# Sink-and-window attention with two mixture-of-experts layers on one core: keys and queries of a pair of heads are turned and split behind the scores of the preceding pair

## Chip, core and metric

The kernel runs on one core of a Trainium2 chip. The metric is the device time of one execution in microseconds (us). It is measured as the median of several runs; the profile is one further execution, with its own time.

The engines of a core work from their own in-order instruction streams: TensorE (PE, matmuls and transposes into PSUM; its weight loads are listed as PEld), VectorE (DVE), ScalarE (ACT), GpSimd (POOL) and SyncE (SP), whose queue issues most DMAs here. Semaphores hold an instruction until what it reads is there.

## What is computed

```python
def _attn_ref(q, k, v, n_sink, window):            # q, k, v: [4, 8, 768, 64]
    scores = scale * np.matmul(q, k.transpose(0, 1, 3, 2))
    is_sink = pos[None, :] < int(n_sink)           # 4 sinks
    rel = pos[:, None] - pos[None, :]
    in_window = (rel >= 0) & (rel < int(window))   # window 128
    scores = np.where(is_sink | in_window, scores, -1000000000.0)
    scores = scores - np.max(scores, axis=-1, keepdims=True)
    a = np.exp(scores)
    a = a / (np.sum(a, axis=-1, keepdims=True) + 1e-09)
    return np.matmul(a, v)
...
def _moe_ref(x, w_in, w_out):                      # 3072 tokens, 512 -> 2048 -> 512
    h = x @ w_in
    g = np.where(h >= 1, h, np.where(h <= -1, 0.0, (h + 1) ** 2 / 4))
    return g @ w_out
...
def reference(**kwargs):
    x = attention, heads side by side: [3072, 512]
    x = _moe_ref(x)
    return _moe2_ref(x)    # 8 experts, each takes its 384 best tokens: relu(x @ w1) @ w2
```

The code is shortened, and the last function is told in words.

## The kernel before

**Tiling.** The 3072 tokens are 12 blocks of 256 (two tiles of 128), three blocks per batch; blocks 0, 3, 6 and 9 begin a batch (`first`, t0 = 0) and have the sinks' loads besides. In a block attention goes over four pairs of heads. Precision comes from splitting a float32 operand into a high and a low part and adding two or three matmuls. Blocks 0 and 1 take `attn_steps_f32`, which turns keys and queries by TensorE transposes (L482, L498); blocks 2 to 11 take `attn_steps`, which turns them by VectorE. Each block's output x is the input of the first dense MoE (`moe1_steps`: `hid` L632, activation L640 to L644, `proj` L657), which runs in between the attention of later blocks; the second MoE follows from about 775 us on.

**The steps of a pair in `attn_steps`.** `load_kq` issues four DMAs for k and eight for q on SP (L427, in `load_blocks`), `load_v` two for v (L276) and, in a first block, four for the sinks' rows (L284). `trans_k` turns k by a VectorE stream transpose (L431), copies its high part on ScalarE (L303), makes the low one on VectorE (L304) and adds the sinks (L308, L309). `trans_q` does the same: transpose (qr, L431), high part sq on ScalarE (L317), low part ql on VectorE (L318). `s00` to `s11` are the scores: two matmuls each (sc, L335 with ql, L336 with sq), the maximum on VectorE (L338), the exponential on ScalarE (L340). `norm` takes the reciprocal on VectorE (L345, L346) and multiplies the probabilities on GpSimd (pr; L354, and L349 and L351 in first blocks). `ptrans` turns them on TensorE (tp, L373) with their high and low part on ScalarE (pt, L375) and VectorE (pt, L376); `strans` does so for the sinks' part. `pv` multiplies with the values (xp, L392), `split` makes x (xa: L398 on ScalarE, L399 on VectorE; then L408 or L411, L412, L413), `split_v` splits the values (L289, L290), `sinks` the sinks' rows (svt L591, L592; sv L596).

**What sets the order.** `pipeline` (L599 to L614) writes the steps of one stage after the other: a stage belongs to a pair, "+" names steps of the next pair and "*" of the one after it. A plan spreads the stages over time among the MoE steps by weights (the steps named in `idle` weigh nothing, except `trans_k` and `trans_q` of blocks 0 and 1, which are on TensorE), and that gives the program's order. The framework's scheduler then orders the instructions of each engine by what is ready and by that program order, so it can already hoist a step past its neighbours. The raw tiles of k, q and v, and ks, sq and ql, have one buffer each; pr, pt and the split values two.

Of the kernel before, what the change touches and what calls it, by code (L numbers as in the profile page):

```python
# [74 lines left out]
class Kernel:  # L75
# [524 lines left out]
    def pipeline(self, pairs):  # L600

        idle = {"load_kq", "load_v", "trans_k", "trans_q", "norm0", "norm1", "split_v", "sinks", "split"}

        def steps(order, now, nxt, far):
            of = {"": now, "+": nxt, "*": far}
            found = [(of[s.rstrip("abcdefghijklmnopqrstuvwxyz_0123456789")], s.lstrip("+*")) for s in order.split()]
            return [(0.0 if s in idle and s not in d.get("on_pe", ()) else 1.0, d[s]) for d, s in found if d and d[s]]

        out = [steps("load_kq load_v trans_k trans_q +load_kq split_v sinks +load_v s00 s01 norm0 s10 s11 norm1",
                     pairs[0], pairs[1], None)]  # L610
        for now, nxt, far in zip(pairs, pairs[1:] + [None], pairs[2:] + [None, None]):
            out.append(steps("+trans_k +trans_q *load_kq ptrans0 ptrans1 strans +s00 +s01 +norm0 pv0 +s10 +s11 +norm1 "
                             "pv1 +split_v +sinks *load_v split", now, nxt, far))
        return out  # L614


# [763 lines left out]
def tile_sink_window_attention__moe__expert_choice(ctx, tc, q, k, v, n_sink, window, w_in, w_out, wg, w1, w2, out):  # L1380
# [10 lines left out]
    def pipeline(general):  # L1391
        with ExitStack() as c0:
# [72 lines left out]
            plan.run()  # L1465

    pipeline(False)
    flag = nc.values_load(K.flag[0:1, 0:1], min_val=0, max_val=1)
    with tc.If(flag):
        with ExitStack() as c0:  # L1470
            K.attn_general(c0.enter_context, xg)
        pipeline(True)
# [32 lines left out]
```

## Time and profile before

| what | before |
|---|---|
| median of 3 runs | 1196.77 us (1194.34 to 1202.54) |
| the profiled execution: time | 1197.53 us |
| the profiled execution: span from first to last instruction | 1195.6 us |
| mean granted TensorE clock, of full speed | 0.976 |
| TensorE busy | 1112.3 us, 93% of the span |
| VectorE busy | 858.5 us, 72% |
| ScalarE busy | 704.2 us, 59% |
| GpSimd busy | 485.5 us, 41% |

The busy times are sums over the whole span, and 2 us lie outside of it. Where TensorE is nearly always busy, a wait of its own counts in full, and one of another engine only if it reaches TensorE. The rows behind the change show waits in the form "engine line waited for: us in total, times, longest us", and a timeline's row has its idle time and what released it in brackets.

### The profile page before, as it was taken

To read this page: it belongs to the slowest core of one execution; us is meant where nothing else is said; L and a number is where in the kernel's file an instruction comes from. 1 tells how busy PE (TensorE), PEld (TensorE's weight loads), DVE (VectorE), ACT (ScalarE), POOL (GpSimd) and SP (SyncE) were. 2 spreads that over 40 slices of the span, in tenths; PEclk is the share of its full clock that TensorE was granted. 3 is DMA by queue.
4 is the path that set the end of the run, shared out by engine and by line. 5 is a ranking of instruction groups with operands and counts; after the bars stand their busy time and mean duration, and the time that the engine had idled before them with its cause. 6 is when DMAs were issued, how large, how long until landed. Compare 5 with 4: busy or idle time off the path is not lost.

```text
span 1195.6 us, 24202 instructions
## 1 busy us (share of the span) xinstructions
PE 1112.3 (93%) x8256; PEld 1027.9 (86%) x8256; DVE 858.5 (72%) x2578; ACT 704.2 (59%) x1602; POOL 485.5 (41%) x588
## 2 busy tenths in 40 slices
PE   5898989999999999999999999999699999999995
PEld 3677878999999999999998999999578788878994
DVE  6778878777777876776777787755788787878330
ACT  5787767666667666775666676642345434444551
POOL 1335645454555444455544455541222222322321
PEclk9899989999999999999999999999799999999998
DMA  4555522323222122222122322000667767677861
GB/s 113 132 154 166 159 50 55 65 48 75 47 55 40 34 55 49 56 50 58 33 52 49 69 42 57 11 19 1 185 173 200 204 168 208 189 192 194 227 176 41
DMA packets 241926, 118.11 MB, mean 99 GB/s; under 512 B 196096, under 2 KB 220672, under 8 KB 241792
## 3 DMA queue, kind: packets, MB, share of 16 engines
q1 hardware_dynamic: 233200, 86.58, 28.5%
q0 software_dynamic: 8592, 29.89, 10.7%
q8 instruction: 67, 1.10, 0.4%
q14 instruction: 67, 0.55, 0.2%
HBM read 86.00 MB, written 13.11 MB: 83 GB/s over the span
## 4 chain that ended last, share of the span: by engine, by line
PE 54%; DVE 10%; issue 8%; ACT 5%; POOL 4%; DMA 3%; SPq 1%; DVEq 0%; POOLq 0%; ACTq 0%
PE up L657 14%; PE hp L632 14%; PE hp L1054 8%; PE us L1081 7%; PE xp L392 2%; PE tp L373 2%; PE sc L335 2%; PE sc L336 1%; DVE ks L304 1%; POOL pr L354 1%; PE pk L955 1%; DVE ind L804 1%; SPq L427 1%; POOL gl L644 1%; PE pg L819 1%
## 5 line engine op out<-in xcount | busy, mean ns | idle before, releaser
L644 POOL TENSOR_TENSOR gl<-u,gh 128x256 fp32r<-128x256 f32 x192 | 148.9, 776 | 210.1 <-ACT gh L643 159.3
L657 PE MATMUL up<-woh,gl 128*128 128x256 f32 (+1 forms) x576 | 167.1, 290 | 2.0 <-POOL gl L644 1.7
L657 PE MATMUL up<-wol,gh 128*128 128x256 f32 (+1 forms) x576 | 164.6, 286 | 0.6 <-DVE wol L231 0.6
L657 PE MATMUL up<-woh,gh 128*128 128x256 f32 x576 | 164.3, 286 | 0.0
L641 ACT ACTIVATE u<-u,half 128x256 f32<-128x256 f32 x192 | 98.0, 510 | 89.6 <-DVE u L640 82.3
L632 PE MATMUL hp<-xh,wil 128*128 128x256 f32 x768 | 132.3, 291 | 3.8 <-ACT xh L412 1.9
L632 PE MATMUL hp<-xl,wih 128*128 128x256 f32 x768 | 125.9, 284 | 0.7 <-POOL xl L413 0.5
L632 PE MATMUL hp<-xh,wih 128*128 128x256 f32 x768 | 126.0, 285 | 0.0
L657 PEld LDWEIGHTS up<-woh,gl 128*128 128x128 f32 x576 | 109.8, 191 | 3.8 <-POOL gl L644 2.3
L632 PEld LDWEIGHTS hp<-xh,wil 128*128 128x128 f32 x768 | 107.4, 191 | 6.2 <-ACT xh L412 2.9
L657 PEld LDWEIGHTS up<-wol,gh 128*128 128x128 f32 x576 | 109.4, 190 | 1.2 <-DVE wol L231 0.8
L657 PEld LDWEIGHTS up<-woh,gh 128*128 128x128 f32 x576 | 109.4, 190 | 0.7 <-issue 0.7
L632 PEld LDWEIGHTS hp<-xl,wih 128*128 128x128 f32 x768 | 106.7, 191 | 1.9 <-POOL xl L413 1.5
L632 PEld LDWEIGHTS hp<-xh,wih 128*128 128x128 f32 x768 | 107.2, 193 | 0.0
L642 DVE TENSOR_TENSOR u<-hp,u 128x256 f32<-128x256 f32 x192 | 80.8, 421 | 33.6 <-ACT u L641 31.9
L640 DVE TENSOR_SCALAR u<-hp 128x256 f32<-128x256 f32 x192 | 80.2, 418 | 34.4 <-PE hp L632 29.3
L354 POOL TENSOR_TENSOR pr<-pr,sm 128x576 f32<-128x576 f32 x56 | 69.3, 1238 | 68.9 <-DVE sm L346 34.6
L340 ACT ACTIVATE pr<-pr,sm 128x288 f32<-128x288 f32 (+1 forms) x160 | 85.5, 535 | 18.3 <-DVE sm L338 17.4
L643 ACT CAST gh<-u 128x256 fp32r<-128x256 f32 x192 | 77.7, 405 | 27.0 <-DVE u L642 24.0
L1062 ACT ACTIVATE hh<-hp 128x384 fp32r<-128x384 f32 x64 | 31.5, 492 | 102.9 <-PE hp L1054 88.3
L376 DVE TENSOR_TENSOR pt<-tp,pt 128x512 fp32r<-128x512 f32 (+1 forms) x80 | 51.5, 647 | 41.8 <-ACT pt L375 41.1
L1081 PE MATMUL us<-w2h,hl 128*128 128x512 f32 x192 | 80.8, 421 | 0.0
(270 smaller groups left out, 3047.8 us busy)
## 6 DMA issues: line engine op xcount, KB each, us to landing
w1r<-in_moe_w_dram SPq DMA_DIRECT2D x32, 512.0 KB, 4.4
w2r<-in_moe_w_dram SPq DMA_DIRECT2D x32, 512.0 KB, 4.6
w2l<-w2r POOLq DMA_DIRECT2D x32, 512.0 KB
qr<-in_q_dram SPq DMA_DIRECT2D x320, 32.0 KB, 2.0
dr<-in_moe_w_in_dram SPq DMA_DIRECT2D x16, 512.0 KB, 4.1
dr<-in_moe_w_out_dram SPq DMA_DIRECT2D x16, 512.0 KB, 4.4
x2d<-ev SPq DMA_DIRECT2D x26, 256.0 KB, 2.2
kr<-in_k_dram SPq DMA_DIRECT2D x112, 48.0 KB, 2.2
```

The lines of the kernel that those rows point to most:

```text
L340: nc.scalar.activation(pr, pr, AF.Exp, bias=sm[:, 0, u:u + 1], scale=-1.0, accum_out=sm[:, 1, u:u + 1])
L354: nc.gpsimd.tensor_tensor(out=pr, in0=pr, in1=r.unsqueeze(2).to_broadcast([P, 2, 2 * P + NS]), op=OP.mult)
L376: nc.vector.tensor_tensor(out=pt[:, 1, :n], in0=ps, in1=pt[:, 0, :n].bitcast(F32), op=OP.subtract)
L632: nc.tensor.matmul(ps, w_[:, k, fs], x_[:, k, :], start=(i == 0 and k == 0), stop=(i == 2 and k == 3))
L640: nc.vector.tensor_scalar(u, ps, -1.0, 1.0, op0=OP.max, op1=OP.min)
L641: nc.scalar.activation(u, u, AF.Square, bias=self.half, scale=0.5)
L642: nc.vector.tensor_tensor(out=u, in0=ps, in1=u, op=OP.max)
L643: nc.scalar.copy(gh, u)
L644: nc.gpsimd.tensor_tensor(out=gl, in0=u, in1=gh.bitcast(F32), op=OP.subtract)
L657: nc.tensor.matmul(o, g_[:, ts], self.w_out_part(w_, f)[:, cs], start=(f == fa and i == 0 and (cs.start > 0 or t == 0)), stop=(f == fz - 1 ...
L1054: nc.tensor.matmul(ps, w_[:, k, fs], x_[:, k, :], start=(i == 0 and k == 0), stop=(i == 2 and k == 3))
L1081: nc.tensor.matmul(us[j], h_[:, o], w_[:, f % 2, :], start=(f == 0 and i == 0), stop=(f == nf - 1 and i == 2))
```

## The change

`trans_k` and `trans_q` of a pair, which stood at the head of the preceding pair's stage beside that pair's transposes, now stand one stage earlier, right behind the last scores and the norm of the pair before (ahead of `pv1`, `split_v` and `load_v`). `load_kq`, which refills their tiles, moves along with them and is now of the third pair ahead ("^"). The first group of steps gets the three for its pairs as well. Nothing within a step changes. In the changed kernel lines after 613 have numbers that are 2 higher (L640 is L642 there).

```diff
-        def steps(order, now, nxt, far):
-            of = {"": now, "+": nxt, "*": far}
-            found = [(of[s.rstrip("abcdefghijklmnopqrstuvwxyz_0123456789")], s.lstrip("+*")) for s in order.split()]
+        def steps(order, now, nxt, far, last):
+            of = {"": now, "+": nxt, "*": far, "^": last}
+            found = [(of[s.rstrip("abcdefghijklmnopqrstuvwxyz_0123456789")], s.lstrip("+*^")) for s in order.split()]
             return [(0.0 if s in idle and s not in d.get("on_pe", ()) else 1.0, d[s]) for d, s in found if d and d[s]]
 
-        out = [steps("load_kq load_v trans_k trans_q +load_kq split_v sinks +load_v s00 s01 norm0 s10 s11 norm1",
-                     pairs[0], pairs[1], None)]
-        for now, nxt, far in zip(pairs, pairs[1:] + [None], pairs[2:] + [None, None]):
-            out.append(steps("+trans_k +trans_q *load_kq ptrans0 ptrans1 strans +s00 +s01 +norm0 pv0 +s10 +s11 +norm1 "
-                             "pv1 +split_v +sinks *load_v split", now, nxt, far))
+        out = [steps("load_kq load_v trans_k trans_q +load_kq split_v sinks +load_v s00 s01 norm0 s10 s11 norm1 "
+                     "+trans_k +trans_q *load_kq",
+                     pairs[0], pairs[1], pairs[2], None)]
+        for now, nxt, far, last in zip(pairs, *(pairs[i:] + [None] * i for i in (1, 2, 3))):
+            out.append(steps("ptrans0 ptrans1 strans +s00 +s01 +norm0 pv0 +s10 +s11 +norm1 "
+                             "*trans_k *trans_q ^load_kq "
+                             "pv1 +split_v +sinks *load_v split", now, nxt, far, last))
```

What stands in the engines' streams is the scheduler's doing, so three places follow as they stand there.

VectorE at the end of block 6, behind the second half's scores of its third pair and ahead of the first scores of its fourth (qr and ql are that pair's queries, ks and sk its keys; pt and xa belong to the pair before). Before:

```order
L345 TENSOR_SCALAR sm<-sm 128x2
L346 RECIPROCAL sm<-sm 128x2
L304 TENSOR_TENSOR ks<-kr,ks 64x2x128
L431 STREAM_TRANSPOSE qr<-qr 128x512
L399 TENSOR_TENSOR xa<-xp,xa 64x384
L592 TENSOR_TENSOR svt<-vr,svt 128x64
L308 CAST sk<-ks 128x64
L376 TENSOR_TENSOR pt<-tp,pt 128x384
L596 TENSOR_SCALAR sv<-svt,par 128x128 x2
L309 CAST ks<-sk 128x2x32
L318 SCALAR_TENSOR_TENSOR ql<-qr,sq 128x512
```

In the changed kernel:

```order
L431 STREAM_TRANSPOSE qr<-qr 128x512
L642 TENSOR_SCALAR u<-hp 128x256
L338 ISA pr,sm<-sc,m_129 128x288
L338 ISA sm 128x1
L304 TENSOR_TENSOR ks<-kr,ks 64x2x128
L644 TENSOR_TENSOR u<-hp,u 128x256
L345 TENSOR_SCALAR sm<-sm 128x2
L346 RECIPROCAL sm<-sm 128x2
L304 TENSOR_TENSOR ks<-kr,ks 64x2x128
L308 CAST sk<-ks 128x64
L309 CAST ks<-sk 128x2x32
L318 SCALAR_TENSOR_TENSOR ql<-qr,sq 128x512
```

The transpose of the queries moved from behind the reciprocal to ahead of the last maximum, and ql now stands ahead of xa, svt, pt and sv, which follow these rows.

VectorE in block 3, behind the keys of its third pair. Before:

```order
L304 TENSOR_TENSOR ks<-kr,ks 64x2x128
L308 CAST sk<-ks 128x64
L309 CAST ks<-sk 128x2x32
L399 TENSOR_TENSOR xa<-xp,xa 64x384
L431 STREAM_TRANSPOSE qr<-qr 128x512
L640 TENSOR_SCALAR u<-hp 128x256
L318 SCALAR_TENSOR_TENSOR ql<-qr,sq 128x512
L642 TENSOR_TENSOR u<-hp,u 128x256
```

In the changed kernel:

```order
L304 TENSOR_TENSOR ks<-kr,ks 64x2x128
L308 CAST sk<-ks 128x64
L309 CAST ks<-sk 128x2x32
L399 TENSOR_TENSOR xa<-xp,xa 64x384
L642 TENSOR_SCALAR u<-hp 128x256
L376 TENSOR_TENSOR pt<-tp,pt 128x384
L644 TENSOR_TENSOR u<-hp,u 128x256
L431 STREAM_TRANSPOSE qr<-qr 128x512
L376 TENSOR_TENSOR pt<-tp,pt 128x384
L592 TENSOR_TENSOR svt<-vr,svt 128x64
L318 SCALAR_TENSOR_TENSOR ql<-qr,sq 128x512
```

Here qr has moved behind a pt and ql behind two of them and svt; on TensorE the scores that read ql stand six up matmuls (L657) further back.

SyncE's queue in block 9 (kr, qr: keys and queries; vr: values and sinks). Before:

```order
L427 DMA kr<-in_k_dram 32x8x32 x4
L427 DMA qr<-in_q_dram 32x8x32 x2
L276 DMA vr<-in_v_dram 128x2x64 x2
L284 DMA vr<-in_v_dram 32x64 x4
L427 DMA qr<-in_q_dram 32x8x32 x6
```

In the changed kernel:

```order
L427 DMA kr<-in_k_dram 32x8x32 x4
L427 DMA qr<-in_q_dram 32x8x32 x8
L276 DMA vr<-in_v_dram 128x2x64 x2
L284 DMA vr<-in_v_dram 32x64 x4
L427 DMA kr<-in_k_dram 32x12x32 x4
```

All eight transfers of the queries now stand ahead of the values' six.

## Rows read from the trace of the kernel before

**Rows 1.** Windows: stretch, length, busy PE PEld DVE ACT POOL, clock, DMA share, GB/s.

```profile
0.00:200.00 200.00, 169.87 (x1086) 146.06 (x1087) 154.87 (x443) 143.41 (x352) 86.16 (x97) 0.93 0.46 121
200.00:775.00 575.00, 550.10 (x4494) 542.81 (x4494) 434.85 (x1220) 385.60 (x979) 290.38 (x362) 1.00 0.26 50
```

**Rows 2.** TensorE's waits from 200 to 775 us: total us, times, longest.

```profile
PE tp L373 <- POOL pr L354: 13.4, 11, 1.9
PE sc L335 <- DVE ql L318: 7.7, 6, 2.1
PE hp L632 <- ACT xh L412: 1.9, 3, 1.1
```

**Rows 3.** Timeline, TensorE: start us, us, instruction, idle before and its releaser.

```profile
277.68 0.40 PE L335 MATMUL sc<-ks,ql 128*128 128x288 f32 x1 [1.48 <-DVE ql L318]
...
446.88 0.33 PE L335 MATMUL sc<-ks,ql 128*128 128x128 f32 x1 [2.07 <-DVE ql L318]
...
464.59 0.40 PE L335 MATMUL sc<-ks,ql 128*128 128x288 f32 x1 [1.17 <-DVE ql L318]
...
634.40 0.33 PE L335 MATMUL sc<-ks,ql 128*128 128x128 f32 x1 [0.99 <-DVE ql L318]
...
650.38 0.40 PE L335 MATMUL sc<-ks,ql 128*128 128x288 f32 x1 [1.13 <-DVE ql L318]
```

**Rows 4.** Timeline, VectorE, ahead of the scores at 446.88.

```profile
442.88 0.71 DVE L431 STREAM_TRANSPOSE qr<-qr 128x512 f32<-128x512 f32 x1 [1.18 <-DMA qr<-in_q_dram]
443.62 0.55 DVE L399 TENSOR_TENSOR xa<-xp,xa 64x384 f32<-64x384 f32 x1
444.20 0.23 DVE L592 TENSOR_TENSOR svt<-vr,svt 128x64 fp32r<-128x64 f32 x1
...
444.72 0.55 DVE L376 TENSOR_TENSOR pt<-tp,pt 128x384 fp32r<-128x384 f32 x1
445.19 0.94 DVE L596 TENSOR_SCALAR sv<-svt,par 128x128 fp32r<-128x128 f32 x2
...
446.15 0.68 DVE L318 SCALAR_TENSOR_TENSOR ql<-qr,sq 128x512 fp32r<-128x512 f32 x1
```

**Rows 5.** Timeline, SyncE's DMA issues, the loads ahead of those scores.

```profile
433.10 0.91 SPq L276 DMA_DIRECT2D vr<-in_v_dram  x2
434.05 2.39 SPq L284 DMA_DIRECT2D vr<-in_v_dram  x4
436.49 3.05 SPq L427 DMA_DIRECT2D qr<-in_q_dram  x6
```

**Rows 6.** Timeline, block 3: VectorE and TensorE at two pairs' first scores.

```profile
233.37 0.69 DVE L318 SCALAR_TENSOR_TENSOR ql<-qr,sq 128x512 fp32r<-128x512 f32 x1 [0.70 <-ACT sq L317]
...
234.82 0.22 PE L335 MATMUL sc<-ks,ql 128*128 128x128 f32 x1
...
246.88 0.52 PE L373 MATMUL tp<-ident,pr 128*128 128x128 f32 x3
...
248.68 0.22 PE L335 MATMUL sc<-ks,ql 128*128 128x128 f32 x1
```

**Rows 7.** Timeline, GpSimd: one pr by itself, one beside a ql.

```profile
312.82 1.16 POOL L354 TENSOR_TENSOR pr<-pr,sm 128x576 f32<-128x576 f32 x1 [0.81 <-DVE sm L346]
...
319.10 1.59 POOL L354 TENSOR_TENSOR pr<-pr,sm 128x576 f32<-128x576 f32 x1 [3.79 <-DVE ks L309]
```

**Rows 8.** The first 200 us: TensorE's waits, and a window (columns of rows 1).

```profile
PE gp L219 <- DVE df L247: 4.1, 6, 1.6
PE gg L227 <- ACT gw L221: 3.1, 2, 2.9
PE up L657 <- POOL wql L249: 2.2, 2, 1.4
...
30.00:40.00 10.00, 9.35 (x38) 6.39 (x38) 9.16 (x38) 8.37 (x25) 4.34 (x8) 0.66 0.42 84
```

**Rows 9.** ScalarE's waits from 200 to 775 us: the cast of the values.

```profile
ACT v L289 <- DMA vr<-in_v_dram: 5.4, 6, 1.6
```

## The prediction

> **What bounds the kernel now.** I read three views, in this order. The table of windows says where TensorE has something to lose or to win [rows 1]. Between 200 and 775 us, where nearly all of attention runs in between the first MoE, TensorE is busy 550.10 of 575 us at a granted clock of 1.00: it bounds this part, it has 24.9 us of idle time, and nothing is to be won from the clock. VectorE, ScalarE and GpSimd are busy 435, 386 and 290 us of it and have slack on average. In the first 200 us TensorE idles 30.1 us at a clock of 0.93. After 775 us no step of attention is left.
>
> TensorE's waits in 200 to 775 us [rows 2] name two steps of attention as nearly the whole: transposes of the probabilities (tp) that wait for GpSimd's normalisation (pr), 13.4 us in 11 waits, and scores (sc) that wait for VectorE's low half of the queries (ql), 7.7 us in 6. The change moves what makes ql; it doesn't move what makes pr. So 7.7 us is about all that it can take out of the steady part directly.
>
> The timeline gives five of the six waits by place [rows 3]: 1.48, 2.07, 1.17, 0.99 and 1.13, together 6.84 us. They stand where a block with t0 = 0 ends and the next begins: for block 6 the last pair's scores (446.88) and the next block's first (464.59), the same for block 9 (634.40, 650.38), for block 3 only the second (277.68). In the other pairs of blocks 4 to 11 the scheduler had put ql early enough: no wait is booked there.
>
> The reason at 446.88 is on VectorE and on the DMA queue. VectorE transposed the queries (qr) at 442.88, after 1.18 us of waiting for their DMA, and then did xa (0.55), pt (0.55) and the sinks' sv (0.94) before ql, which ended at 446.83 [rows 4]; the score matmul went 0.05 later. The queries came late because SyncE issued two of their eight transfers, then six for values and sinks (0.91 and 2.39 us), then the other six of the queries (3.05) [rows 5].
>
> **The change part by part.** It removes and adds no instruction, and every price below is one of order.
>
> *The five waits.* In the new order of VectorE at 446.88 ql is ahead of xa, svt, pt and sv, and qr stands ahead of the last score's reduction instead of behind the reciprocal. Work of 0.55 + 0.55 + 0.94 = 2.04 us moves behind ql, and the queries' transfers move ahead of the values' six, 3.30 us, against the 1.18 us for which VectorE waited for them. Both exceed what is needed for 2.07 us between them, so this wait goes. At 464.59 the new order has qr right behind the reciprocal and ql ahead of both pt, svt and sv: more than 1.17 us. The other three stand in the same pattern. I take all five: **-6.8 us**. The sixth, some 0.9 us at the end of block 2 (7.7 less 6.84), stays.
>
> *Block 3.* Here the new order is worse. At the scores of 248.68 it puts a pt ahead of qr, and a second pt and svt ahead of ql. The transposes behind the first pt were issued at 246.88 and took 0.52 [rows 6]. By the durations of [rows 4], with 0.5 for ScalarE's copy: 247.40 + 0.5 + 0.55 for pt, 0.4 for u, 0.71 for qr, 0.63 for sq on ScalarE and 0.68 for ql is 250.9 (0.5, 0.4 and 0.63 are my estimates, by operations on tiles of the same size). The score matmul moves back by six up matmuls of 0.12 (0.7 us), to 249.4: a new wait of 1.5 us. One pair earlier ql began at 233.37 and the scores at 234.82 [rows 6], 0.76 us of slack. Two instructions, pt and u (1.0), now go first, and the transposes' and sq's wait add 0.7: 0.9 over the slack, less what the scores move back, some 0.6. I take 0.3. Together **+1.8 us**, between 0 (scores move back further than I count) and 3.6 (both twice as large).
>
> *xa, pt and sv behind ql.* xa feeds the split of x, for which hid waits 1.9 us in three waits [rows 2]. Its cover is a whole stage of matmuls. I take **0**; the bound is that it doubles, +1.9.
>
> *GpSimd's pr beside ql.* In seven stages ql newly goes right behind the reciprocal, ahead of xa, when GpSimd does pr. Of two pr of one shape the one alone took 1.16 us, the one that ql ran beside 1.59 [rows 7], so 7 x 0.43 = 3.0 us of longer pr. The transposes at these seven places do not wait for pr now; the eleven waits of [rows 2] stand elsewhere, where the order stays. I take **0**, bound +3.0. The Trainium skill, "SBUF — State Buffer", section "SBUF: two separate sides", makes it a lock: a VectorE operation with two SBUF inputs and a GpSimd operation exclude each other for the whole instruction. ql has two such inputs, so by that rule a pr would lose all of ql's time; the rows here show less, 0.43 where a ql takes 0.68, and by the rule the sum would be some 1197 rather than 1192.
>
> *The loads.* Per pair four k and eight q transfers move ahead of the v transfers on SyncE's queue. In the twelve pairs of the blocks with t0 = 0 six of the queries' go past six of the values': v comes 3.05 us later [rows 5]. The cover is a stage, since values are split a stage behind their load: at 434.05 + 2.39 = 436.44 the last was issued, and svt used it at 444.20, 7.8 us later [rows 4, 5]. A landing takes no more than 3.3 us (the queries issued until 439.54 were transposed at 442.88), which leaves 4.5, more than 3.05. I take **0**. The bound is a rival below.
>
> *The front.* Blocks 0 and 1 use TensorE transposes; there the change moves matmuls too, and up to about 218 us TensorE's order is reshuffled between attention, weight decode and the first MoE steps. The view of waits has 4.1 (gp), 3.1 (gg) and 2.2 us (up) for decoded weights there [rows 8]. A new order can save these 9.4 us, or lose: the stretch from 30 to 40 us has a granted clock of 0.66 (part of it at 1.2 GHz), so 10 x 0.34 = 3.4 us for one more such stretch, 6.8 for two. What brings the first weights and the first keys is unchanged, so I take **0**, from -9.4 to +6.8.
>
> Sum against the profiled execution: 1197.5 - 6.8 + 1.8 = 1192.5 us. It stands 0.8 above the median of the three runs shown (1196.8), so 1191.7: **1192 us**. Its own range, by block 3's and the small bounds (-1.8 and +1.8, +1.9), is 1188 to 1196.
>
> **The rivals.**
>
> *The waits pass on.* The scores start earlier, but GpSimd's pr takes the place: its waits grow in the seven stages, by 3.0 us (1195), or by 7 x 0.68 = 4.8 us if pr and ql wholly exclude each other (1196.5); or ql's place is held by its ScalarE half, and nothing changes (1197). For it: pr is already the largest wait, 13.4 us. Against: the five places of ql and most of the seven are different stages.
>
> *Values late (the other side).* If v's transfers are late by those 3.05 us, ScalarE's cast of v waits, and behind it on ScalarE the copies of pt and the exponentials. ScalarE waits now for v 5.4 us in 6 waits, 1.6 at most [rows 9]. Twelve pairs at 1.6 us give 19 us, 1211; the gain of 5.0 us is eaten at 0.42 us each, which is the point from which it decides. In between, say 1 us each, is 1204. Against it: the cover of a stage worked out above.
>
> *The front gains.* If the three waits for weights go, 9.4 us less: 1182.
>
> *The front loses.* One or two more stretches at the lower clock: 1195 to 1198.
>
> **How the numbers follow.** Forecast 0.48 (1188 to 1196); passed on or nothing 0.20 (1195 to 1198); front gains 0.14 (1181 to 1187); front loses 0.11 (1195 to 1200); values late 0.07 (1197 to 1211). The range 1183 to 1202 leaves out about half of the front's gain (0.06) and most of the late values (0.05). A measurement of this kernel can tell about 1% (12 us) from no change; its three runs span 8 us. Faster by over 1% is below 1184.8: most of the front's gain, 0.10. Slower by over 1% is above 1208.7: the far half of the late values and more than two clock stretches, 0.05. The rest, 0.85, is within 1%.
>
> **What would show it.** Right: in 200 to 775 us TensorE's idle time falls from 24.9 to about 20, the waits of sc for ql from 7.7 in 6 to about 2.7 in 3 (the one at the end of block 2 and two in block 3), and those of tp for pr stay at 13 to 14 in 11; on SyncE eight q transfers stand together ahead of v. Wrong: tp for pr grows to 16 or more (passed on); waits of ScalarE for v grow from 5.4 towards 19 (values late); the 0 to 200 us part changes its TensorE idle time or its clock by more than 3 us (front). If block 3's two waits do not come, the time is 1190.

## The result

The changed kernel took 1190.6 us in the median of 13 runs, beside 1202.5 us for the kernel before in the same group of runs: a ratio of 0.991, 95% interval 0.989 to 0.993. In a later group it was 1190.7 against 1198.5 (0.992, 0.990 to 0.995). So it is 8 to 12 us faster, about twice the 5 us of the forecast, and inside 1%. The profiled execution took 1191.5 us with a span of 1189.7, where that of before took 1197.5 and 1195.6.

The windows of the changed kernel, columns as in [rows 1]:

```profile
0.00:200.00 200.00, 173.81 (x1141) 148.69 (x1142) 158.59 (x450) 145.80 (x359) 89.78 (x100) 0.97 0.47 123
200.00:775.00 575.00, 552.64 (x4490) 545.40 (x4489) 437.90 (x1219) 383.27 (x978) 290.49 (x360) 0.99 0.25 49
```

In the first 200 us TensorE is busy 3.9 us longer and the granted clock is 0.97 instead of 0.93. From 200 to 775 us idle time falls from 24.9 to 22.4 us, and the clock is 0.99, no longer 1.00.

TensorE's waits of the changed kernel from 200 to 775 us, beside [rows 2]:

```profile
PE tp L373 <- POOL pr L354: 14.3, 11, 2.0
PE sc L335 <- DVE ql L318: 2.9, 5, 0.9
PE hp L634 <- POOL xl L413: 2.3, 2, 1.2
PE hp L634 <- ACT xh L412: 1.5, 4, 0.5
```

The waits for ql fell from 7.7 to 2.9 us. Those for pr grew by 0.9 us, and the matmul hp now waits for xl, 2.3 us where it was 0.5 before.

To see where the time went I compare the start of the same instruction in both traces: VectorE's reduction of a score tile (L338), 160 in each. At 207 us the changed kernel is 4.3 us ahead, at 267 us 3.8, at 763 us 6.0, and from there to the end it stays about 6. So most of what this pair of profiles shows was gained in the front, where I had put 0.

TensorE's waits of the changed kernel in the first 200 us, beside [rows 8]:

```profile
PE hp L634 <- POOL wil L249: 3.1, 5, 0.9
PE up L659 <- POOL gl L646: 2.9, 4, 1.1
...
PE gg L227 <- ACT gw L221: 1.4, 1, 1.4
...
PE up L659 <- POOL wql L249: 0.7, 1, 0.7
...
PE gp L219 <- DVE df L247: 0.4, 1, 0.4
```

The three waits named in [rows 8] went from 9.4 to 2.5 us, and others grew: hp for wil, 3.1 us where it was 0.2, and up for gl, 2.9 where it was 1.7. Summed over windows of 2.5 us as (1 - granted clock) x 2.5, the lower of the two clock levels (1.2 instead of 2.4 GHz) cost 13.7 us in the first 200 us of the profile of before and 6.8 in that of the changed kernel. Up to the L338 instruction at 267.3 us (263.4 in the changed kernel) that sum fell by 6.9 us and TensorE's idle time by 3.1, from 32.0 to 28.9, while its busy time without that sum grew by 6.2; together they are the 3.8 us. So this pair of profiles alone doesn't say whether the clock or the waits made the gain.

### The profile page after: what moved, and what is told of

The parts are those of the page before. It is cut to its first block, busy times and chain, and to the rows that moved or that the text cites. A ratio compares the mean times of both kernels' runs of the same rounds, so it can differ in the third digit from the quotient of the medians.

```text
span 1189.7 us, 24247 instructions
## 1 busy us (share of the span) xinstructions
PE 1113.0 (94%) x8256; PEld 1027.3 (86%) x8256; DVE 862.4 (72%) x2578; ACT 701.3 (59%) x1602; POOL 487.4 (41%) x588
## 4 chain that ended last, share of the span: by engine, by line
PE 58%; DVE 13%; issue 10%; ACT 6%; POOL 5%; DMA 4%; SPq 2%; DVEq 0%; POOLq 0%; ACTq 0%
PE hp L634 15%; PE up L659 14%; PE hp L1056 8%; PE us L1083 7%; PE xp L392 2%; PE tp L373 2%; PE sc L335 1%; DVE u L642 1%; PE sc L336 1%; POOL pr L354 1%; SPq L427 1%; DVE ks L304 1%; PE pk L957 1%; ACT u L643 1%; PE sc L517 1%
## 5 line engine op out<-in xcount | busy, mean ns | idle before, releaser
L642 DVE TENSOR_SCALAR u<-hp 128x256 f32<-128x256 f32 x192 | 80.1, 417 | 40.4 <-PE hp L634 32.2
L340 ACT ACTIVATE pr<-pr,sm 128x288 f32<-128x288 f32 (+1 forms) x160 | 85.2, 533 | 20.2 <-DVE sm L338 19.7
```

Of the source, the lines that this page charges most:

```text
L340: nc.scalar.activation(pr, pr, AF.Exp, bias=sm[:, 0, u:u + 1], scale=-1.0, accum_out=sm[:, 1, u:u + 1])
L642: nc.vector.tensor_scalar(u, ps, -1.0, 1.0, op0=OP.max, op1=OP.min)
```

## Experiments

For every profile I give two things from the traces: how far it stands from the first profile of before at three of those L338 instructions (minus is ahead), and what the lower clock cost in two parts by the sum just described. The last two columns are means over all runs of a kernel and not of one profile: (1 - mean granted clock) x span, and the run's time less that. They cover the whole execution, so the first is larger than the sums of the parts; it also counts time in which TensorE idles. For before they are taken over its 78 runs in the three later groups. "Steady order" is that of blocks 3 to 11. All values are us but the ratio.

| kernel | ratio to before | 207 us | 267 us | 763 us | clock, 0 to 200 | clock, 265 to 780 | clock, all runs | rest, all runs |
|---|---|---|---|---|---|---|---|---|
| before, first profile | 1 | 0 | 0 | 0 | 13.7 | 1.7 | 28.1 | 1170.1 |
| before again | 0.9995 | -0.8 | -1.0 | -1.9 | 10.2 | 1.7 | 26.9 | 1170.7 |
| steady order only | 0.995 | +3.0 | +3.7 | -3.9 | 13.7 | 1.7 | 27.8 | 1163.8 |
| changed, first profile | 0.991 | -4.3 | -3.8 | -6.0 | 6.8 | 5.1 | 23.9 | 1166.3 |
| changed again | 0.992 | -6.3 | -5.8 | -6.4 | 3.4 | 6.8 | 24.2 | 1166.5 |
| front only | 0.9955 | -7.5 | -7.1 | -7.6 | 1.7 | 1.7 | 20.1 | 1171.5 |
| block 0 only | 0.9965 | -7.1 | -6.8 | -4.2 | 1.7 | 5.1 | 23.1 | 1171.6 |
| block 1 only | 0.996 | -3.1 | -2.5 | -2.6 | 6.8 | 1.7 | 26.8 | 1168.0 |
| changed, late loads | 0.9885 | -6.7 | -6.3 | -12.7 | 5.1 | 0 | 15.6 | 1168.2 |
| queries only, late loads | 0.985 | -6.8 | -6.4 | -14.5 | 3.4 | 1.7 | 17.7 | 1163.1 |
| queries only, early loads | 0.977 | -8.4 | -7.7 | -28.6 | 0 | 0 | 17.5 | 1153.7 |
| changed, tp later | 0.999 | -6.2 | -5.6 | -5.0 | 5.1 | 1.7 | 19.7 | 1176.4 |
| changed, tp later, late loads | 0.998 | -7.0 | -6.6 | -4.0 | 1.7 | 3.4 | 19.4 | 1177.1 |
| changed, slower pr | 1.010 | -4.9 | -3.2 | +16.6 | 3.4 | 15.4 | 29.2 | 1182.2 |

**Both kernels once more.** No edit.

> The kernel before once more, with nothing changed. Two readings of the change's result stand against each other. A: the profile of before happened to be a quick execution, and single executions differ by how many stretches run at the lower TensorE clock; then this run's times lie between 1194 and 1206 us and go with their mean clock, a thousandth of the clock being worth about 1.2 us (a thousandth of the span). B: the kernel before takes the same work at the same clock in about 1202, and something besides the clock differs. In both the ratio to before is 1.000 within 0.002.

> The changed kernel once more, beside the others of this group. Its ratio to before was 0.991; the same here, within 0.002, some 1187 to 1191 us if before is 1197. Its stretches at a lower clock between 265 and 780 us, three in the first profile, are between 0 and 3, all behind waits of 1.86 us or more, if such waits bring them about by chance; if the order itself fixes them they are the same three.

Before: 1196.5 us (ratio 0.9995, 0.997 to 1.002), runs from 1194 to 1203. Changed: 1190.7 us (0.992). Reading A holds: over the 78 runs the time goes with the mean granted clock (correlation 0.93), 1.2 us for a thousandth as A had it. Of the changed kernel's stretches at the lower clock, those at 315 and 656 us came in both profiles, the one at 503 us only in the first, two at 349 and 472 us only in the second. That is four where I had written at most three, and those two came behind two or three shorter waits close together (0.45 to 1.16 us), not behind one of 1.86 or more. So in these profiles many places stay the same, and the execution decides which of them fall.

**Where the gain is.** The order strings of a group of blocks are chosen by its first block:

```diff
-                steps = K.pipeline([p for b in blks for p in (...)(b, xtiles)])
+                steps = K.pipeline([p for b in blks for p in (...)(b, xtiles)], blks[0] < 3)   # front only
+                # steady order only: blks[0] >= 3; block 0 only: blks[0] == 0; block 1 only: blks[0] == 1
```

> The change in blocks 0 to 2 alone; blocks 3 to 11 keep the order of before. Theory 1 (front): the profiles show the changed kernel 4.3 us ahead at about 207 us, so this kernel is 4 to 7 us faster than before and keeps the five waits of the scores for ql between 270 and 660 us (6.8 us in all). Theory 2 (steady part): the front's 4.3 us are chance of two single executions; then it is within 2 us of before.

> The change in blocks 3 to 11 alone; blocks 0 to 2 keep the order of before. Theory 1 (front): the five waits go (about 7 us to about 3 us in all for scores waiting for ql), but part comes back as a lower clock behind waits of the transposes for pr of about 2 us, so 2 to 5 us faster than before. Theory 2 (steady part): it has the whole gain of the change, 9 to 12 us.

> The change in block 0 alone (queries and keys turned by TensorE transposes), all else as before. The front-only kernel gained 5.4 us, and the profiles show 1.7 to 6.8 us lost to a lower clock in the first 200 us where the order of before loses 10.2 to 13.7. If block 0's order does it, 4 to 6 us faster than before with at most 7 us lost to the clock; if block 1's does, within 2 us of before.

> The change in block 1 alone, all else as before. The counterpart to the kernel with the change in block 0 alone: if block 1's order does it, 4 to 6 us faster than before with at most 7 us lost to the clock in the first 200 us; if block 0's does, within 2 us of before. Both halves may also gain some of it each, 2 to 3 us.

Front only: 1191.9 us, ratio 0.9955 (0.993 to 0.998). Steady order only: 1192.1 us, 0.995 (0.993 to 0.9975). Each half brings some 5 us and together they are the change, so theory 1 holds and theory 2 falls. Front only keeps five waits for ql (5.8 us in all); with the steady order only none is left from 265 to 775 us. Blocks 0 and 1 bring 0.3 to 0.4% each, 0.9965 (0.994 to 0.999) and 0.996 (0.994 to 0.999). Block 0's time (1193.6, 4.9 us below before) is that of "block 0's order does it", but block 1 alone brings 3.7 us as well, more than either of its readings gave for that case, so the front's gain belongs to neither alone.

The front's gain is the clock. Over their runs front only loses 20.1 us to it and before 28.1, and the rest of the time is not lower (1171.5 and 1170.1). At 207 us the nine profiles with the changed front shown in the table (single blocks aside) stand 4.3 to 8.4 us ahead and lose 0 to 6.8 us to the clock; the three with the order of before stand 0.8 ahead to 3.0 behind and lose 10.2 to 13.7. Why the new order brings fewer such stretches isn't shown. From 25 to 206 us TensorE's longest wait is 2.9 to 3.5 us in those three (the gate's matmul gg) and at most 1.4 in the nine; but block 0 only loses just 1.7 us there with waits of up to 2.3, and in the first profile of the changed kernel a stretch at 33 us has no wait over 0.3 us in the 9 us ahead of it.

In the steady part, from 267 to 763 us, the three profiles with the changed order gain 2.2, 0.6 and 7.6 us, where the five with the order of before (block 0 only and block 1 only among them) stand between 0.9 ahead and 2.6 behind. With the clock's cost taken out of both, the three gain 7.3, 7.4 and 9.3 us and the five 1.7 to 2.6, so the order is worth some 5.8 us, and the clock gave back a part of it in two of the three. All runs agree: with the steady order only the rest falls from 1170.1 to 1163.8 us and the clock's cost stays (27.8 and 28.1). What the changed kernel gives back shows against front only, 24 us in the mean of its 24 runs beside 20.1.

**Long waits and the clock.** The windows of the changed kernel around its longest wait for pr:

```profile
310.00:315.00 5.00, 3.95 (x33) 3.75 (x32) 4.53 (x13) 4.86 (x12) 1.38 (x3) 1.00 0.10 17
315.00:320.00 5.00, 4.07 (x21) 4.00 (x22) 2.17 (x4) 2.02 (x6) 3.92 (x5) 0.66 0.47 75
320.00:325.00 5.00, 5.00 (x43) 5.00 (x43) 2.99 (x11) 2.34 (x7) 0.81 (x2) 1.00 0.19 44
```

In front of the fall stands a wait in the timeline of TensorE:

```profile
315.93 0.39 PE L373 MATMUL tp<-ident,pr 128*128 128x128 f32 x1 [1.99 <-POOL pr L354]
```

The stretch cost 5 x 0.34 = 1.7 us on top of the 1.99 of the wait. A wait of 1.95 us in the profile of before, which ended at 508 us, was not followed by one:

```profile
505.00:510.00 5.00, 3.05 (x26) 2.85 (x25) 4.55 (x10) 3.71 (x9) 3.87 (x4) 1.00 0.21 36
```

To test it, the waits were lengthened:

```diff
                     nc.gpsimd.tensor_tensor(out=pr, in0=pr, in1=r.unsqueeze(2).to_broadcast([P, 2, 2 * P + NS]),
                                             op=OP.mult)
+                    nc.gpsimd.tensor_scalar(pr[:, 0, :P], pr[:, 0, :P], 1.0, None, op0=OP.mult)
```

> The changed kernel with GpSimd's normalisation lengthened by one more operation, a multiplication of half of one tile by 1.0, some 0.5 us, wherever a block has no t0 = 0; values are unchanged. Theory C (a wait of about 2 us brings the clock down): the waits of tp for pr grow by about 0.5 us each, five or more are above 1.9 us, and four or more stretches between 265 and 780 us have the lower clock, 1.7 us each; in all 8 to 14 us slower than the changed kernel. Rival (the lower clock is not tied to these waits): the stretches stay between 0 and 3, and the time goes up by the waits alone, 4 to 7 us.

It took 1211.5 us, 21 us above the changed kernel. TensorE's waits from 265 to 775 us, and one window:

```profile
PE tp L374 <- POOL pr L356: 25.1, 13, 3.4
PE hp L635 <- ACT xh L413: 2.2, 4, 0.7
```

```profile
575.00:580.00 5.00, 2.40 (x13) 2.25 (x12) 3.63 (x6) 3.14 (x7) 4.91 (x6) 0.71 0.27 46
```

The waits for pr grew by 11 us (the changed kernel has 13.9 in these windows), and 15.4 us were lost to seven stretches at the lower clock, against 5.1 in three. Theory C holds, and the loss is larger than I wrote. This profile is the slowest of the six runs, though: in the mean of all six the clock costs 5.2 us more than in the changed kernel, and the rest, waits above all, 15.8 more. In all the profiles here each stretch between 265 and 780 us came behind waits of TensorE of 1.6 to 3.4 us, single or two or three close together in sum; waits of 1.5 to 2.3 us also passed without one.

**Later transposes.** With the clock in mind I moved the second half's transposes, which wait for pr, and those of the sinks' part behind the next pair's first two scores, in blocks 3 to 11:

```diff
-ptrans0 ptrans1 strans +s00 +s01 +norm0 pv0 ...
+ptrans0 +s00 +s01 ptrans1 strans +norm0 pv0 ...
```

> The changed kernel, but in blocks 3 to 11 the second half's transposes of the probabilities and the sinks' transposes stand behind the next pair's first two scores. Lower clock behind waits (theory C): of the profiles so far, stretches at a lower clock between 265 and 780 us begin only behind a wait of TensorE of 1.86 us or more, about every second time, 1.7 us each. Then this order takes most of the 14 us of waits of tp for pr out, none is left above 1.8 us, the clock is 1.00 from 265 to 780 us, and the time is 8 to 14 us below the changed kernel. Rival D: what GpSimd is late with is then waited for elsewhere (by pv for pt, or by the split of x), the waits of 200 to 775 us keep their sum near 18 us, and the time is within 4 us of the changed kernel.

> The same two later transposes, with the loads of keys and queries at the head of the next stage in blocks 3 to 11, as in the kernel before (the earlier kernel with late loads took 1183.8 us). If the two add up: 1172 to 1180. If the loads' place gained only by shortening waits of tp for pr below 1.8 us, which are gone here anyway: as the kernel with later transposes and early loads, within 3 us of it.

Neither gained: 1195.9 (0.999, 0.9965 to 1.0015) and 1196.0 us (0.998, 0.996 to 1.001), 5 us above the changed kernel. TensorE's waits of the first from 265 to 775 us:

```profile
PE sc L343 <- DVE ql L326: 13.6, 12, 2.0
PE xp L400 <- DVE st L374: 3.9, 8, 1.0
PE hp L640 <- ACT xh L420: 3.4, 4, 1.4
PE hp L640 <- POOL xl L421: 2.8, 3, 1.2
```

No wait for pr is left, and the 14 us stand at the scores, which now come before ql is ready. Rival D holds in kind: what is late is waited for elsewhere. The waits sum to 23.7 us, more than its 18, and the time is 5 us above the changed kernel, not within 4. Moving these steps of TensorE did not help the pair's chain. The second kernel is within 3 us of the first, as its second reading had it, with 17.3 us of waits for ql.

**Which part of the change works, and the loads.** Three orders for blocks 3 to 11, all with the changed front ("late loads" also has the front's loads late):

```diff
 changed:                     ptrans0 ... +norm1 *trans_k *trans_q ^load_kq pv1 ...
 late loads:         *load_kq ptrans0 ... +norm1 *trans_k *trans_q pv1 ...
 queries, late:  +trans_k *load_kq ptrans0 ... +norm1 *trans_q pv1 ...
 queries, early: +trans_k *load_k  ptrans0 ... +norm1 *trans_q ^load_q pv1 ...
```

> The change with the loads of keys and queries left at the head of the next stage, as in the kernel before, so that keys and queries are turned early in the program but loaded as late as before. If the place of trans_k and trans_q does the work in the steady part, the waits of the scores for ql stay as in the changed kernel (about 3 us) and the time is that of the changed kernel. If the place of the loads does it, the five waits are back (about 7 us, the one near 441 us 1 to 2 us long), and the time is that of the front-only kernel, a few us above the changed kernel.

> Front as changed; in blocks 3 to 11 only the queries are turned behind the scores, the keys at the head of the next stage as before, and the loads there too. If the queries' turn is what the scores waited for, the waits of sc for ql between 265 and 780 us are as low as with both moved (about 3.7 us with late loads) and the time is 1183 to 1187. If the keys' work on VectorE, which stands ahead of ql, has to move as well, they are 5 to 7 us as in the front-only kernel, and the time is 1189 to 1193.

> Front as changed; in blocks 3 to 11 only the queries are turned behind the scores, and their loads are issued there as well, while keys are loaded and turned at the head of the next stage. The kernel with both loads at the head took 1180.9 us and has 4.3 us of waits of sc for ql left. If late query loads are the cause of the two near 442 and 458 us (1.3 and 1.2), they go, and the time is 1176 to 1180. If VectorE's own order is the cause, they stay and the time is 1180 to 1184.

Late loads: 1183.8 us, 0.9885 (0.986 to 0.991). Queries only, late loads: 1180.9, 0.985 (0.981 to 0.989). Queries only, early loads: 1170.9, 0.977 (0.974 to 0.980), the fastest of all, 20 us below the changed kernel. TensorE's waits from 265 to 775 us with late loads:

```profile
PE tp L373 <- POOL pr L354: 11.7, 9, 1.5
PE sc L335 <- DVE ql L318: 3.7, 5, 1.4
PE hp L634 <- ACT xh L412: 2.6, 3, 1.5
```

Queries only, late loads:

```profile
PE tp L381 <- POOL pr L362: 5.2, 8, 1.0
PE sc L343 <- DVE ql L326: 4.3, 5, 1.3
PE hp L640 <- ACT xh L420: 2.2, 2, 1.6
```

Queries only, early loads:

```profile
PE tp L387 <- POOL pr L368: 2.5, 3, 1.3
PE sc L349 <- DVE ks L318: 1.3, 2, 0.9
PE hp L646 <- ACT xh L426: 1.0, 1, 1.0
```

I had not expected late loads to be faster than the changed kernel; both readings there fall. Its waits sum to about what the changed kernel's do (18.4 and 19.2 us), but none is longer than 1.54 us, and its profile has no stretch at the lower clock from 265 to 780 us. Over its five runs the whole gain is the clock: 15.6 us instead of 24, with a rest that is 1.8 us higher. Queries only, late loads, has the waits for ql near the 3.7 us expected (4.3), and its time is 2 us below the range given.

How the keys' move can cost time shows in the timeline of one pair. It is one place, and no kernel moved the keys alone; between the two with early loads the keys' turn and the keys' loads differ together, and between the two with late loads, where only the turn differs, the intervals overlap. The changed kernel, ScalarE, VectorE and GpSimd, behind a score that ended at 497.2:

```profile
498.27 0.50 ACT L303 CAST ks<-kr 64x384 fp32r<-64x384 f32 x1
...
499.08 0.56 ACT L340 ACTIVATE pr<-pr,sm 128x288 f32<-128x288 f32 x1
...
499.85 0.16 DVE L345 TENSOR_SCALAR sm<-sm 128x2 f32<-128x2 f32 x1
500.12 0.71 DVE L431 STREAM_TRANSPOSE qr<-qr 128x512 f32<-128x512 f32 x1
500.76 0.12 DVE L346 RECIPROCAL sm<-sm 128x2 f32<-128x2 f32 x1
...
501.50 1.47 POOL L354 TENSOR_TENSOR pr<-pr,sm 128x576 f32<-128x576 f32 x1
```

The cast of the keys goes ahead of the last exponential on ScalarE, and the transpose of the queries between the two steps of the norm on VectorE. GpSimd starts pr 4.3 us behind the score, and tp waits 1.91 us. The same pair with queries only and early loads, behind a score that ended at 486.3:

```profile
487.56 0.55 ACT L354 ACTIVATE pr<-pr,sm 128x288 f32<-128x288 f32 x1
...
488.11 0.50 ACT L317 CAST ks<-kr 64x384 fp32r<-64x384 f32 x1
488.23 0.17 DVE L359 TENSOR_SCALAR sm<-sm 128x2 f32<-128x2 f32 x1
488.43 0.17 DVE L360 RECIPROCAL sm<-sm 128x2 f32<-128x2 f32 x1
...
488.74 1.47 POOL L368 TENSOR_TENSOR pr<-pr,sm 128x576 f32<-128x576 f32 x1 [2.39 <-ACT ks L317]
```

Here the queries were done before, the keys follow the exponential, and pr starts 2.5 us behind the score; tp does not wait. The loads matter for the queries: with late ones VectorE's qr at 439.16 still waits 1.16 us for its DMA, and the scores at 442 us wait 1.31; with early ones both are gone. The gain of that is more than either reading gave, and it is all in the rest: 1153.7 us beside 1163.1, at the same cost of the clock.

## Why the prediction was right, and where not

- **The five waits (-6.8).** Right in kind and nearly in size. With the steady order only all five went, and TensorE's idle time from 200 to 775 us fell to 19.8 us, the 20 of the forecast; in the changed kernel it is 22.4. At the end of block 6 the scores stand without a wait, and SyncE's queue shows the cause foreseen, the queries' transfers ahead of the values':

```profile
427.69 3.41 SPq L427 DMA_DIRECT2D qr<-in_q_dram  x7
431.35 0.90 SPq L276 DMA_DIRECT2D vr<-in_v_dram  x2
432.30 2.39 SPq L284 DMA_DIRECT2D vr<-in_v_dram  x4
```

  Four waits went; the one of 1.48 us behind block 3 was halved:

```profile
271.60 0.40 PE L335 MATMUL sc<-ks,ql 128*128 128x288 f32 x1 [0.73 <-DVE ql L318]
```

  So 6.1 instead of 6.8 us, in waits.
- **Block 3 (+1.8).** Near in sum, but not for the reason given. Waits of 0.73, 0.94 and 0.33 us stand there, less the 0.90 of before that went: +1.1. The one I worked out as 1.5 measured 0.94, the one of 0.3 a pair earlier measured 0.15, and the other two were not foreseen. The rows of VectorE ahead of the 0.94, in the order foreseen:

```profile
242.04 0.70 DVE L431 STREAM_TRANSPOSE qr<-qr 128x512 f32<-128x512 f32 x1
242.97 0.56 DVE L376 TENSOR_TENSOR pt<-tp,pt 128x384 fp32r<-128x384 f32 x1 [0.23 <-ACT pt L375]
243.44 0.22 DVE L592 TENSOR_TENSOR svt<-vr,svt 128x64 fp32r<-128x64 f32 x1
243.65 0.69 DVE L318 SCALAR_TENSOR_TENSOR ql<-qr,sq 128x512 fp32r<-128x512 f32 x1
```

  These waits come with the front, not with the steady order: with the steady order alone, which has block 3's new order, only one of 0.9 us stands there, the one that before has too, and front only, with block 3 as before, has 0.72, 0.94 and 1.05. So the new order of block 3 that the prediction blamed is not what costs, and the agreement in size is luck.
- **xa behind ql (0, bound +1.9).** It cost, inside the bound but by another order: the sum of hp's waits went from 2.4 to 3.8 us. The new ones are 0.43 for xh at 470.0 and 1.17 us for xl at 471.9. There VectorE's xa (467.88) still stands ahead of ql, though behind qr, and GpSimd does gl and the values' low part before xl; before, xl followed its xa directly:

```profile
469.44 0.72 POOL L646 TENSOR_TENSOR gl<-u,gh 128x256 fp32r<-128x256 f32 x1
470.12 1.01 POOL L290 TENSOR_TENSOR v<-vr,v 128x384 fp32r<-128x384 f32 x1
471.08 0.73 POOL L413 TENSOR_TENSOR xl<-xa,xh 128x256 fp32r<-128x256 f32 x1
```

- **pr beside ql (0, bound +3.0).** Right in sum: the 50 large multiplications take 62.7 us where they took 62.4. The waits for pr grew by 0.9 us. By the exclusive lock of the Trainium skill ("SBUF — State Buffer", "SBUF: two separate sides") they should have grown with each ql moved beside one; the sum of pr's durations here does not show it. Single ones do lengthen, by less than a ql: of the 56 in each trace ql runs beside 10 before and 15 in the changed kernel (for 0.1 us or more), and these took 1.43 and 1.46 us in the mean, where those with neither ql nor ks beside them took 1.16. The pr of 1.59 us in [rows 7] had xa beside it too, behind ql. The sum hardly grew because fewer of the others stand beside ks, 4 instead of 11.
- **Values late (0).** Right: the rival, by which ScalarE's waits for v would grow, falls. They fell instead, from 5.4 us in 6 to 2.0 in 2.
- **The front (0).** This is the step that failed. It is worth about 5 us of the 8 to 12, and the sign named for it came: in the first 200 us TensorE's idle time fell by 3.9 us and the clock's cost by 6.9. Its rival had the gain as waits for weights. Those went from 9.4 to 2.5 us, but other waits grew, and the gain came from stretches at the lower clock that no longer occur. I had priced such stretches on the side of the loss alone, though the order of before had six of them in its profile.
- **The clock in the steady part.** I wrote that nothing was to be won or lost there, because it read 1.00. It gave back 3.4 us in the first profile of the changed kernel and 5.1 in the second, behind waits for pr that the change left, some a little longer (1.54 became 1.99 at the first), and, at 349 and 472 us, behind hp's waits for xh and xl. That the steady order by itself brings them isn't shown: with it alone the clock cost no more than before, 27.8 us over its runs.

Two readings of the prediction were off besides. The bounds that it names give 1190 to 1195, not 1188 to 1196; and attention does not end at 775 us, the last pair's pv and split run until 786.6.

So the steady part's forecast is borne out in size (-5.0; steady order only measured -5.0), with 2.0 us more of hp's waits there in the place of block 3's. That the time came within 1.4 us of 1192 is luck in part. The front's 5 us were missed, and against them stood two things: a reference of three runs (1196.8, where 1202.5 and 1197.0 to 1198.5 were measured in larger groups) and the clock, which takes some 4 us more from the changed kernel than from front only.

## What to carry to other kernels

Add up waits with what follows them: in this kernel a TensorE wait near 2 us in an otherwise busy stretch could cost another 1.7 us of lower clock, so look for long single waits before many short ones, and read the clock window by window, in the slow places too. Compare the mean granted clock over all runs as well, since one profile is one draw. When two steps are moved together, move each alone: here the queries alone, with early loads, gained 1.5% more than queries and keys together. A step moved ahead to feed one wait stands in front of another chain on the same engines; moving the waiting step only carried the wait along here.

## What was unexpected of the hardware

In the steady part TensorE is busy over 95% of the time, and still the granted clock fell for a stretch behind single waits of 1.6 to 2.1 us, in some executions and not in others, at 1.7 us each. The spread of this kernel's runs (1190.6 to 1206.6 us for 78 of before) goes with the mean granted clock, 1.2 us for a thousandth. With fewer long waits the spread was smaller, 1168.5 to 1174.5 us for the fastest version, though in six runs only.
